# Top-k attention and a gated feed-forward in one kernel: the reciprocal sums are turned by a DMA transpose instead of TensorE

## The chip, the cores and the metric

The kernel runs on one core of one Trainium2 chip. A core has a matrix engine (TensorE, PE in the profile; its weight loads are PEld), a vector engine (VectorE, DVE), an activation engine (ScalarE, ACT), a general engine (GpSimd, POOL) and a queue processor that here issues nearly all DMAs (SyncE, SP). Each runs its own instruction list in order[...]. The metric is the device time of one execution in microseconds (us). Before the change it is 1482.66 us, the median of 3 runs (1482.02 to 1483.18).

## The reference

Two blocks in a row. The attention block has 8 batches of 8 heads, 576 positions and head size 64:

```python
scores = scale * np.matmul(q, k.transpose(0, 1, 3, 2))
kth = np.partition(scores, -top_k, axis=-1)[..., -top_k:-top_k + 1]   # top_k = 32
scores = np.where(scores >= kth, scores, -1000000000.0)
attn = np.exp(scores - np.max(scores, axis=-1, keepdims=True))
attn = attn / (np.sum(attn, axis=-1, keepdims=True) + 1e-09)
attn_out = np.matmul(attn, v)
```

Its output, laid out as 4608 tokens of 512 features, goes through a feed-forward block: `h = x @ w_in` (512 to 2048), `g = h / (1 + exp(-1.702 h))`, `out = g @ w_out` (2048 to 512). All is float32.

## The kernel before, in words

**Slots.** The attention work is cut into 144 slots of 128 query rows by two heads: per batch 16 full slots (four row blocks by four head pairs) and two slots of tails, each of 64 rows of two head pairs. A slot goes through these steps, each on another engine: scores on TensorE (L283), copied to SBUF by ScalarE (L295); the 32 largest of each row by VectorE, with eight-at-a-time maxima and replacements (L345, L348), after the two halves of a row are paired into a larger and a smaller one (L324 on VectorE, L327 and L328 on GpSimd); the bounds of the row by GpSimd (L378); masking and exponentials on ScalarE (L398, L401), which also leave the sum of each row; a copy that parts the float32 probabilities into 16-bit halves (L471); a DMA to DRAM (L473) and a transposing DMA back (L479), which gives `pt`, the probabilities with keys on the partitions; the product with v on TensorE (L539, `values_at`).

**The sums.** The product is made with unnormalised probabilities, so it has to be multiplied by the reciprocal of the row sums, which by then lie along the columns. `sums_of` keeps the sums of a pair of slots in one small tile, 128 x 4. `invert` adds 1e-9 (L430), takes the reciprocal (L432), and lets GpSimd repeat each of the four numbers 64 times into `wide` (L434); `sum_rows` turns `wide` on TensorE, one 128x128 transpose for each slot (L528), into the same PSUM tile `o` that the products go to. ScalarE copies `o`, sums and products together, to SBUF as `x` (L924), and GpSimd multiplies the two parts into the feed-forward's input `xT` (L553, `x_of`).

**The feed-forward.** Four head pairs of one row block make a tile of 128 tokens, which `finish_x` appends to the list `ready`. `hidden` takes the first of that list and makes 512 of its 2048 hidden features (L587, 32 matrix instructions); ScalarE applies tanh (L604) and copies h (L607), GpSimd gates (L616, L617), and `project` multiplies by `w_out` (L635, 8 matrix instructions), four of which add up to one output tile (L641 to SBUF, L643 to DRAM).

**The order.** It is written out by hand (a manual schedule): an engine runs its instructions in the order in which the functions below are called. Slots 0 to 12 go one at a time (`slot`, with another way of turning the probabilities). From slot 13 on `two_slots(n)`, n odd, is called once for every two slots, called a round here. 66 of the rounds finish a pair of slots. In a round, in program order: loads that are due (`begin`); bounds, exponentials and split of slot n-1; the top-k of slot n (`find(n)`, with `invert` of the pair before inside it, after the ninth operation); one `hidden`, one `project`; in 24 of the rounds `prepare_by_dma`, which splits a pair of q and k (L241) and sends it out by four DMAs (L245, L249, L250); the two transposes of `sum_rows`; the scores of slot n+2; the products of slots n-3 and n-2 (`values_at`); the transposing DMA of slot n-1 and, after `prepare_by_dma`, that of q and k (L254); scores of n+3; then more due loads, the bounds and exponentials of slot n, with the copy of `o` and the multiplications `x_of` between them; the split and the transposing DMA of slot n; a second `hidden` and `project`; and the top-k of slot n+1. The SP queue takes its DMAs in just this order, and one that waits holds back all behind it.

**Buffers.** The pool `raws` has 8 buffers that rotate among `lesser`, `wide`, `h`, `x` and others; `ptp` has two (`pt`); `ps_t`, in PSUM, has two (`o` and one `ph`).

Of the kernel before, what the change touches and what calls it, by code (L numbers as in the profile page):

```python
# [11 lines left out]
F32 = mybir.dt.float32  # L12
U32 = mybir.dt.uint32
I32 = mybir.dt.int32
U16 = mybir.dt.uint16
PSUM = bass.MemoryType.PSUM
DRAM = bass.MemoryType.DRAM

P = 128
# [11 lines left out]
def kernel(  # L31
# [27 lines left out]
    nc = tc.nc  # L59

    B, H, S, D = q.shape
# [29 lines left out]
    pool = lambda name, bufs, **kw: ctx.enter_context(tc.tile_pool(name=name, bufs=bufs, **kw))  # L91
# [11 lines left out]
    thp = pool("thp", 5)  # L103
    apart = pool("apart", 4, space=DRAM)
    apart_qk = pool("apart_qk", 2, space=DRAM)
    ps_s = pool("ps_s", 2, space=PSUM)
    ps_t = pool("ps_t", 2, space=PSUM)
    ps_h = pool("ps_h", 1, space=PSUM)
# [309 lines left out]
    def sums_of(n):  # L418
# [3 lines left out]
            sums[k] = small.tile([P, 2, 2], F32, name="sums")  # L422
        return sums[k][:, n % 2, :]

    def invert(n):

        k = n // 2
        if k in sums:
            total = sums[k][:]
            nc.vector.tensor_scalar_add(total, total, 1e-9)  # L430
            inverse = small.tile([P, 4], F32, name="inverse")
            nc.vector.reciprocal(inverse[:], total.rearrange("p s j -> p (s j)"))  # L432
            wide = sums[k] = raws.tile([P, 2, 2, D], F32, name="wide", tag="raw")
            nc.gpsimd.tensor_copy(  # L434
                out=wide[:].rearrange("p s j d -> p (s j) d"),
                in_=inverse[:].unsqueeze(2).to_broadcast([P, 4, D]),
            )

    def turn(n, first, blocks):
        pr = st[n]["pr"]  # L440
# [82 lines left out]
            put_off.append(bring)  # L523


    def sum_rows(m, to):

        nc.tensor.transpose(to, sums[m // 2][:, m % 2, :, :], ident[:])  # L528

    def values_at(m, o):  # L530

        b, t, hps = slots[m]
# [12 lines left out]
                    )  # L545
        st[m].clear()

    def x_of(m, o, by):

        b, t, hps = slots[m]  # L550
        for p in range(2 if t == NF else 1):
            cols = slice(p * TAIL, (p + 1) * TAIL) if t == NF else slice(0, P)
            nc.gpsimd.tensor_tensor(out=x_at(b, t, hps[p]), in0=o[:, cols], in1=by[:, cols], op=ALU.mult)  # L553
        finish_x(m)
# [297 lines left out]
    def two_slots(n):  # L852

        first, second = [later.pop(m, []) for m in (n, n + 1)]
        live = lambda m: 0 <= m < N
        aside = n < N

        def begin(todo):
            for fn, args in todo:
                if fn is not prepare and fn is not prepare_by_dma:  # L860
                    fn(*args)

        def prepare_some(todo):
            for fn, args in todo:
                if fn is prepare or fn is prepare_by_dma:
                    fn(*args)

        def find(m):
            for i, op in enumerate(topk_of_pairs(m) if live(m) else [lambda: None] * 23):
                op()  # L870
                if i == 8 and m % 2:
                    invert(m - 2)
                if i > 1 and unfinished:
                    finish_one()

        def project_one():
            if may_project(0):
                project(True)

        def measure(m):  # L880
            if live(m):
                bounds(m)
            gate(aside)

        opens = n == SETTLED + 1
        begin(first)
        measure(n - 1)
        if opens:
            scores(n + 2)
            bring_all()  # L890
        if live(n - 1):
            exponentials(n - 1)
            split(n - 1)
        if opens:
            copy_scores(n + 2)
            tanh(aside)
        find(n)
        hidden(ps_t if opens else None)
        project_one()
        tanh(aside)  # L900
        prepare_some(first)
        held = [m for m in (n - 3, n - 2) if live(m) and "rows" in st[m]]
        o = ps_t.tile([P, 2, 2, P], F32, name="o", tag="tp") if held else None
        for i, m in enumerate(held):
            sum_rows(m, o[:, i, 0, :])
        if live(n + 2) and not opens:
            scores(n + 2)
            copy_scores(n + 2)
        leave_all()
        for i, m in enumerate(held):  # L910
            values_at(m, o[:, i, 1, :])
        if live(n - 1):
            turn_by_dma(n - 1)
        while turns:
            turns.pop(0)()
        if live(n + 3):
            scores(n + 3)
        begin(second)
        measure(n)
        def bring():  # L920
            if not held:
                return
            x = raws.tile([P, 2, 2, P], F32, name="x", tag="raw")
            nc.scalar.copy(out=x[:], in_=o[:])  # L924
            for i, m in enumerate(held):
                x_of(m, x[:, i, 1, :], x[:, i, 0, :])

        if live(n):
            exponentials(n, bring)
        else:  # L930
            bring()
        if live(n):
            split(n)
            turn_by_dma(n)
        hidden(ps_t)
        if live(n + 3):
            copy_scores(n + 3)
        tanh(aside)
        prepare_some(second)
        project_one()  # L940
        leave_all()
        find(n + 1)
# [41 lines left out]
```

## Time and profile before

| | |
|---|---|
| median of 3 runs | 1482.66 us |
| the profiled execution: its time, its span | 1482.51 us, 1480.7 us |
| PE busy | 1442.7 us (97%) |
| DVE busy | 1382.9 us (93%) |
| ACT busy | 1177.6 us (80%) |
| POOL busy | 859.2 us (58%) |
| L528, transposes of the sums: matrix instructions, mean | 132, 273 ns |
| L434, GpSimd's repeat: instructions, mean | 66, 396 ns |
| L924, copy of `o`: instructions, mean | 66, 585 ns |
| packets of the DMA queue, share of 16 engines | 61.6% |

The span runs from the first to the last instruction of the profiled execution; its time has 1.8 us more around it. A mean is the time of one instruction from its start to its end: matrix instructions overlap, so that a row of them takes less than their number times the mean, and the chain of work that ended last shows what each adds. "Busy" of an engine counts an instruction that is blocked inside as well. The releaser that stands beside an idle time is the instruction whose end let the engine go on.

### The profile page before, as it was taken

To read this page: it belongs to the slowest core of one execution; us is meant where nothing else is said; L and a number is where in the kernel's file an instruction comes from. 1 tells how busy PE (TensorE), PEld (TensorE's weight loads), DVE (VectorE), ACT (ScalarE), POOL (GpSimd) and SP (SyncE) were. 2 spreads that over 40 slices of the span, in tenths; PEclk is the share of its full clock that TensorE was granted. 3 is DMA by queue.
4 is the path that set the end of the run, shared out by engine and by line. 5 is a ranking of instruction groups with operands and counts; after the bars stand their busy time and mean duration, and the time that the engine had idled before them with its cause. 6 is when DMAs were issued, how large, how long until landed. Compare 5 with 4: busy or idle time off the path is not lost.

```text
span 1480.7 us, 31436 instructions
## 1 busy us (share of the span) xinstructions
PE 1442.7 (97%) x10784; PEld 1056.0 (71%) x10784; DVE 1382.9 (93%) x4541; ACT 1177.6 (80%) x1865; POOL 859.2 (58%) x1119
## 2 busy tenths in 40 slices
PE   7789899999999999999999999999999999999998
PEld 5667656777777777777777777777777777777776
DVE  7999989999999999999999999999999999999920
ACT  7998688878788887888878797888878798777730
POOL 3777545566655665666656556665565566665610
PEclk8899999999999999999999999999999999999999
DMA  8451256767667676776678686675767766545430
GB/s 245 135 156 51 72 159 180 202 172 179 173 181 201 159 196 179 178 189 178 170 180 200 168 193 171 183 195 163 179 175 203 174 187 184 140 131 132 127 87 15
DMA packets 516321, 242.20 MB, mean 164 GB/s; under 512 B 452672, under 2 KB 490560, under 8 KB 516160
## 3 DMA queue, kind: packets, MB, share of 16 engines
q1 hardware_dynamic: 515728, 239.89, 61.6%
q8 instruction: 85, 1.39, 0.4%
q14 instruction: 76, 0.62, 0.1%
q10 hardware_dynamic: 432, 0.30, 0.1%
HBM read 45.09 MB, written 102.24 MB: 99 GB/s over the span
## 4 chain that ended last, share of the span: by engine, by line
PE 88%; DVE 10%; ACT 2%; issue 0%; POOL 0%; POOLq 0%; ACTq 0%; DVEq 0%
PE ph L587 34%; PE po L635 32%; PE o L539 10%; PE s_ps L283 10%; DVE top L305 4%; DVE left L308 3%; PE o L528 1%; DVE top L345 1%; PE tp L449 1%; DVE wout L153 0%; DVE left L348 0%; PE none L170 0%; DVE greater L324 0%; ACT pr L401 0%; DVE win L153 0%
## 5 line engine op out<-in xcount | busy, mean ns | idle before, releaser
L635 PE MATMUL po<-wout,th 128*128 128x512 f32 x1152 | 518.6, 593 | 1.1 <-ACT ob L641 1.1
L587 PEld LDWEIGHTS ph<-xT,win 128*128 128x128 f32 x4096 | 472.1, 192 | 53.8 <-issue 52.2
L587 PE MATMUL ph<-xT,win 128*128 128x128 f32 x4096 | 484.4, 277 | 0.0
L635 PEld LDWEIGHTS po<-wout,th 128*128 128x128 f32 x1152 | 208.0, 190 | 211.0 <-issue 208.5
L345 DVE MAX8 top<-left 128x8 f32<-128x288 f32 x792 | 325.2, 445 | 0.0
L471 ACT COPY sc<-pr 128x2304 uint16<-128x2304 uint16 x132 | 278.8, 2112 | 4.2
L295 ACT ACTIVATE sc<-s_ps 128x576 f32<-128x576 f32 x288 | 170.9, 646 | 130.2 <-PE s_ps L283 130.2
L328 POOL TENSOR_TENSOR lesser<-lesser,greater 128x576 int32<-128x576 int32 x132 | 186.2, 1411 | 126.5 <-DVE greater L324 126.3
L348 DVE MATCH_REPLACE8 left<-top,left 128x288 f32<-128x288 f32 x528 | 229.6, 442 | 0.0
L401 ACT ACTIVATE pr<-sc,low 128x576 f32<-128x576 f32 x288 | 220.7, 772 | 0.0
L398 ACT ACTIVATE sc<-sc,cut 128x576 f32<-128x576 f32 x288 | 207.2, 772 | 12.4 <-DVE cut L357 5.8
L345 DVE MAX8 top<-lesser 128x8 f32<-128x288 f32 x528 | 213.5, 444 | 0.0
L327 POOL TENSOR_TENSOR lesser<-sc 128x576 int32<-128x576 int32 x132 | 187.0, 1417 | 2.4 <-ACT sc L295 2.4
L283 PE MATMUL s_ps<-qk_t 64*128 64x288 f32 (+1 forms) x1280 | 183.2, 433 | 0.3 <-ACT qk_t L219 0.3
L617 POOL TENSOR_TENSOR th<-th,h 128x512 f32<-128x512 f32 x128 | 163.7, 1279 | 10.7
L378 POOL TENSOR_SCALAR low<-cut,top 128x1 f32<-128x1 f32 x264 | 65.7, 265 | 175.6 <-DVE cut L357 174.1
L324 DVE TENSOR_TENSOR greater<-sc 128x576 f32<-128x576 f32 x132 | 153.8, 1165 | 11.7 <-ACT sc L295 5.5
L539 PE MATMUL o<-pt,v_l 128*64 128x128 f32 (+1 forms) x2368 | 144.4, 265 | 0.0
L539 PEld LDWEIGHTS o<-pt,v_l 128*64 128x64 f32 x2368 | 120.6, 138 | 25.7 <-issue 22.9
L604 ACT ACTIVATE th<-ph 128x512 f32<-128x512 f32 x144 | 85.9, 596 | 54.9 <-PE ph L587 48.3
L283 PEld LDWEIGHTS s_ps<-qk_t 64*128 64x128 f32 (+1 forms) x1280 | 99.4, 178 | 41.0 <-issue 23.1
L348 DVE MATCH_REPLACE8 left<-top,greater 128x288 f32<-128x288 f32 x264 | 114.7, 442 | 0.0
(86 smaller groups left out, 1535.7 us busy)
## 6 DMA issues: line engine op xcount, KB each, us to landing
rows<-sc SPq DMA_DIRECT2D x132, 576.0 KB, 3.2
qk_rows<-halves SPq DMA_DIRECT2D x48, 256.0 KB, 2.8
qk_l<-in_q_dram SPq DMA_DIRECT2D x64, 128.0 KB, 2.9
raw<-in_moe_w_in_dram SPq DMA_DIRECT2D x16, 512.0 KB, 4.9
v_l<-in_v_dram SPq DMA_DIRECT2D x32, 256.0 KB, 3.1
raw<-in_moe_w_out_dram SPq DMA_DIRECT2D x16, 512.0 KB, 3.5
out_dram<-ob SPq DMA_DIRECT2D x32, 256.0 KB, 2.9
qk_l<-in_k_dram SPq DMA_DIRECT2D x62, 128.0 KB, 2.9
```

The source lines that it names most:

```text
L283: nc.tensor.matmul(ps[i][rows, c, 0:HALF], lhsT=qT[b, hps[p]][on, cols], rhs=kT[b, hps[p]][on, FIRST[i] + c * HALF : FIRST[i] + (c + 1) * ...
L295: nc.scalar.mul(out=to, in_=ps[i][:, :, 0:HALF], mul=SCALE)
L327: nc.gpsimd.tensor_tensor(out=whole, in0=a.bitcast(I32), in1=b.bitcast(I32), op=ALU.add)
L328: nc.gpsimd.tensor_tensor(out=whole, in0=whole, in1=greater[n][:].bitcast(I32), op=ALU.subtract)
L345: nc.vector.max(found(r, i, True), src[:, i, :])
L348: nc.vector.match_replace(to[:, i, :], found(r, i), src[:, i, :], LOWEST)
L398: nc.scalar.activation(sc[:, i, :], sc[:, i, :], AF.Prelu, bias=cut[:, i : i + 1], alpha=HUGE)
L401: nc.scalar.activation(pr[:, i * S : (i + 1) * S], sc[:, i, :], AF.Exp, bias=low[:, i : i + 1], accum_out=den[:, i : i + 1],)
L471: nc.scalar.copy(out=halves, in_=pr[:].bitcast(U16).rearrange("p (k h) -> p h k", h=2))
L539: nc.tensor.matmul(o[j * D : (j + 1) * D, cols], lhsT=main[:, j, c, :] if c < NF else tail[:, j, :], rhs=pt[:, MAIN[j] + c if c < NF else ...
L587: nc.tensor.matmul(ph[:, i * tiles * P : (i + 1) * tiles * P], lhsT=win[:, c, f * P : (f + 1) * P], rhs=xT[c], start=(c == 0), stop=(c == ...
L635: nc.tensor.matmul(po[:], lhsT=gT[:, i * P : (i + 1) * P], rhs=wout[:, f, :], start=(f == 0), stop=(f == FC - 1))
```

## The change

The reciprocal of the pair's four sums is still taken by VectorE and repeated by GpSimd, but as 16-bit halves: `wide` is now 128 x 512 of 16 bits instead of 128 x 256 of 32. A DMA writes it to a new DRAM tile (`by_rows`, pool `apart_by`, two buffers), and a transposing DMA (`turn_inverses`) brings it back as `by_t`, with the numbers of both slots along the columns, interleaved. `x_of` multiplies by `by_t` from there. `sum_rows` and its two transposes are gone, and the PSUM tile `o`, the copy of it and `x` are half as wide. `invert` moves too: it was called in `find` of the odd slot n, after the ninth operation, for the pair finished one round earlier; it is now called in `find` of the even slot n+1, after the seventeenth operation (the two first maxima of the smaller halves, behind `pair_up`), for the pair of the same round. The write to DRAM is the last DMA of a round; the transposing one stands behind `values_at`, before that of slot n-1, in the next round.

```diff
+    inverses = {}
+
     def invert(n):
         k = n // 2
-        if k in sums:
-            total = sums[k][:]
-            nc.vector.tensor_scalar_add(total, total, 1e-9)
-            inverse = small.tile([P, 4], F32, name="inverse")
-            nc.vector.reciprocal(inverse[:], total.rearrange("p s j -> p (s j)"))
-            wide = sums[k] = raws.tile([P, 2, 2, D], F32, name="wide", tag="raw")
-            nc.gpsimd.tensor_copy(
-                out=wide[:].rearrange("p s j d -> p (s j) d"),
-                in_=inverse[:].unsqueeze(2).to_broadcast([P, 4, D]),
-            )
+        if k not in sums:
+            return
+        total = sums.pop(k)[:]
+        nc.vector.tensor_scalar_add(total, total, 1e-9)
+        inverse = small.tile([P, 4], F32, name="inverse")
+        nc.vector.reciprocal(inverse[:], total.rearrange("p s j -> p (s j)"))
+        wide = raws.tile([P, 2, 2, 2, D], U16, name="wide", tag="raw")
+        nc.gpsimd.tensor_copy(
+            out=wide[:],
+            in_=inverse[:].bitcast(U16).rearrange("p (s j h) -> p s h j", s=2, h=2).unsqueeze(4).to_broadcast([P, 2, 2, 2, D]),
+        )
+        rows = inverses[k] = apart_by.tile([P, 2, 2, P], U16, name="by_rows")
+        nc.sync.dma_start(rows[:], wide[:].rearrange("p s h j d -> p s h (j d)"))
+
+    def turn_inverses(n):
+        rows = inverses[n // 2]
+        by = inverses[n // 2] = raws.tile([P, P, 2], F32, name="by_t", tag="raw")
+        nc.sync.dma_start_transpose(
+            out=by[:].rearrange("p q s -> p (q s)").bitcast(U16), in_=rows[:].rearrange("q s h c -> (q s h) c")
+        )
...
-    def sum_rows(m, to):
-        nc.tensor.transpose(to, sums[m // 2][:, m % 2, :, :], ident[:])
...
-    def x_of(m, o, by):
+    def x_of(m, o):
         b, t, hps = slots[m]
+        by = inverses[m // 2][:, :, m % 2]
...
         def find(m):
...
-                if i == 8 and m % 2:
-                    invert(m - 2)
+                if i == 16 and m % 2 == 0:
+                    invert(m - 1)
...
-        o = ps_t.tile([P, 2, 2, P], F32, name="o", tag="tp") if held else None
-        for i, m in enumerate(held):
-            sum_rows(m, o[:, i, 0, :])
+        o = ps_t.tile([P, 2, P], F32, name="o", tag="tp") if held else None
...
         for i, m in enumerate(held):
-            values_at(m, o[:, i, 1, :])
+            values_at(m, o[:, i, :])
+        if held:
+            turn_inverses(n - 2)
         if live(n - 1):
             turn_by_dma(n - 1)
...
-            x = raws.tile([P, 2, 2, P], F32, name="x", tag="raw")
+            x = raws.tile([P, 2, P], F32, name="x", tag="raw")
             nc.scalar.copy(out=x[:], in_=o[:])
             for i, m in enumerate(held):
-                x_of(m, x[:, i, 1, :], x[:, i, 0, :])
+                x_of(m, x[:, i, :])
```

More of the change, by code (lines that the diff above doesn't have):

```diff
@@ L105 @@
     apart_qk = pool("apart_qk", 2, space=DRAM)
+    apart_by = pool("apart_by", 2, space=DRAM)
     ps_s = pool("ps_s", 2, space=PSUM)
```

## The prediction, made before the changed kernel was run

> **What bounds the kernel now.** I read the busy times by stretch first, then the chain of work that ended last, then the timeline of one round (one call of `two_slots`) engine by engine. Between 240 and 1400 us TensorE is busy in all of every 40 us and VectorE in 39.3 to 39.6, so either could be the limit. The chain decides: 88% of it is PE. Of its order in time, one whole round:
>
> ```profile
> 610.42 0.22 PE o L528 x2
> 610.64 1.17 PE s_ps L283 x8
> 611.81 2.33 PE o L539 x40
> 614.14 1.17 PE s_ps L283 x8
> 615.31 3.77 PE ph L587 x32
> 619.08 3.44 PE po L635 x8
> 622.52 3.57 PE ph L587 x32
> 626.09 3.44 PE po L635 x8
> 629.52 0.22 PE o L528 x2
> ```
>
> The columns are start, length, engine, tile, line and count. A round lasts 19.10 us (610.42 to 629.52), all of it TensorE with no hole, and L528, which the change removes, is 0.22 us of it: not two means of 273 ns, since matrix instructions overlap.
>
> Why does VectorE, nearly full, not appear? From the timeline, around the multiplication that makes `xT`:
>
> ```profile
> 652.46 0.58 ACT L924 COPY x<-o 128x512 f32<-128x512 f32 x1
> 653.12 0.88 POOL L553 TENSOR_TENSOR xT<-x 128x128 f32<-128x128 f32 x2 [1.48 <-ACT x L924]
> 653.41 2.83 PE L587 MATMUL ph<-xT,win 128*128 128x128 f32 x23
> 653.95 1.41 POOL L327 TENSOR_TENSOR lesser<-sc 128x576 int32<-128x576 int32 x1
> 654.46 1.51 DVE L324 TENSOR_TENSOR greater<-sc 128x576 f32<-128x576 f32 x1
> ```
>
> L324 takes 0.76 us in the first half of nearly every round, but 1.4 to 2.0 in the second, where it starts while GpSimd's L327 runs and ends some 0.6 us after it. L327 follows `x_of`, `x_of` the copy L924, and that TensorE's products. So VectorE is held to TensorE's pace by this stretch of about 0.85 us; alone it would need 19.10 - 0.85 = 18.25 us a round.
>
> The same lines show the tight place. The second `hidden` (653.41) starts 0.29 us after `x_of` does. Each block of `xT` it takes costs two L587, 3.57/32 x 2 = 0.22 us; the two blocks from this round are the third and fourth, needed at about 653.9 and 654.1; they are ready at 653.56 and 654.0. Matching `ready` by its order with the starts of L587, nine tiles are used like this, in the round that makes them (starts 233, 271, 309, 348, 577, 615, 653, 692 and 921 us). All others wait 15 us or more, a round of TensorE's work.
>
> The DMAs by line, kilobytes and median us from issue to landing, and what SP waits for:
>
> ```profile
> rows<-sc SPq DMA_DIRECT2D x132, 576.0 KB, 3.2
> pt<-rows SPq DMA_TRANSPOSE x132, 4.6
> qk_rows<-halves SPq DMA_DIRECT2D x24, 64.0 KB, 2.5
> SPq L479 <- DMA rows<-sc: 307.4, 109, 4.3
> ```
>
> **What the Trainium skill says.** "SBUF — State Buffer", section "SBUF: two separate sides": VectorE and GpSimd share a port pair under an exclusive lock, held for a whole instruction, which also covers a VectorE operation with two SBUF inputs against a GpSimd one that reads SBUF. L324 against L327 agrees (0.76 against 1.51 us). "DMA: Bandwidth & Descriptors", section "Rules for kernel authors": a DMA that reads what another wrote must wait for its completion. The trace agrees: that wait alone is 307.4 us of SP in 109 times, and the change adds one more per round. "Advanced Engine Details and Errata", section "X-Bar Transpose (TRN2)": transposing DMAs are as fast as plain ones. Only partly here: 4.6 us against 3.2 for the same bytes, and the difference lies near the 2.05 to 3.5 us (median 2.49) that SP spends issuing it, against 0.39.
>
> **The change part by part.**
>
> *TensorE.* Two transposes go: -0.22 us a round. In the first three of the 66 rounds other engines lead (below); 63 x 0.22 = -13.9 us. Removing them hides nothing and frees nothing else on TensorE; the weight loads lie under the matrix instructions.
>
> *ScalarE.* L924 is half as wide: about -0.24 us (0.585 to some 0.35, as the 128x384 and 128x128 copies take 0.478 and 0.256 us). ScalarE is 80% busy, so this is worth nothing by itself, but `x` is ready 0.24 us earlier.
>
> *VectorE.* L430 and L432, 0.35 us, move from the first half to the second, one pair earlier. In the steady rounds the sums wait for nothing: the exponentials of slot n end about 2.2 us after the products, the new place comes 4.4 us after. Behind it stand 20 operations of the next cut, and 0.85 us of slack cover 0.35.
>
> *GpSimd.* The repeat is 512 elements, not 256: 0.62 us by L616's 128x512 (617 ns), between 0.40 (L434, if 16-bit elements go twice as fast) and 1.2. It leaves the first half and comes after L328 in the second, where GpSimd now idles 1.3 us waiting for the cut, so I take nothing.
>
> *SP.* Two DMAs more a round. The write is 128 KB: 0.45 us of issue (L473 and L245: 0.33 to 0.6), 2.5 to 2.8 to landing by the rows above. The transpose has 128x512 elements where `pt` has 128x2304: 2.49 x 512/2304 = 0.55 us of issue, floor 0.35, ceiling 2.5 if the count matters little; landing 2.2 us after the issue ends (`pt`: 4.6 - 2.49), so about 2.8 in all, 2.5 to 5. SP's other transposes are at the earliest 1 us from being late: `pt` of slot n lands some 3 us or more before its product.
>
> *The new wait.* `x_of` now also waits for `by_t`. The write leaves after SP's last transpose, about 10.3 us after the products (12.5 beside a transpose of q and k), lands 2.7 later, and in ordinary rounds the transpose lands 1 to 2 us before `x_of` wants it: nothing. In two kinds of round SP is late. With q and k loads due, six loads and often three of v hold SP until the split's DMA is out (e.g. 649.32 + 0.59, products done at 652.28). With 0.5 us for the new write, `by_t` is issued at 650.4 and lands at 653.2 to 653.7. With `prepare_by_dma`, four DMAs go first (to 612.35, products at 614.07), and it lands at 615.2 to 616. Both are 1 to 2 us after the products, where `x_of` used to start 0.84 after. Behind `x_of` on GpSimd stand L327, L328, the repeat, the bounds, and the gate (1.41 + 1.41 + 0.62 + 0.50 + 1.90 = 5.84 us); TensorE wants the gated tile only 11.95 us after the products, so `x_of` may end 6.1 after and costs nothing, except for the nine tiles used at once. All nine are in rounds of these two kinds. There `x_of` must start by 0.95 us after the products; `by_t` comes at 0.9 to 2.3. I take 0.6 us each, 9 x 0.6 = +5.4, from 0 to 1.5 each (+13.5).
>
> *The start.* In the round that begins near 176 us the new place of `invert` meets unfinished exponentials:
>
> ```profile
> 198.91 0.81 DVE L345 MAX8 top<-lesser 128x8 f32<-128x288 f32 x2
> 199.11 0.76 ACT L401 ACTIVATE pr<-sc,low 128x576 f32<-128x576 f32 x1
> 199.78 0.19 ACT L401 ACTIVATION_READ_ACCUMULATOR pr<-sc,low 128x1 f32 x1
> ```
>
> VectorE could start L430 at 198.07 and would wait until 199.97, here on the chain (196.66 to 219). With 0.34 us from L528 and 0.24 from the copy that is 1.67 us, minus 0.68 for two rounds' L528 on the same chain (0.34 each, where they don't overlap): +1.0. One round earlier the wait is 5.4 us (174.4 to 179.8), but 0.85 and 4.62 us of waits for scores swallow it.
>
> Sum: -13.9 + 5.4 + 1.0 = -7.5, from 1482.51 (span 1480.7 and 1.8 around it): 1475.0. The median, 1482.66, stands 0.15 higher; I keep 1475.
>
> *Buffers.* `raws` hands out seven a round instead of six, from eight. Each is then taken when its holder one round and one place earlier is done; the tightest is `h`, after the last read of `lesser`, some 6 us before. No wait.
>
> **The rivals.** (1) *Hidden entirely.* `by_t` lands within 0.95 us of the products in the nine rounds too, or VectorE runs ahead: where `x_of` is late, L324 comes before L327 and loses its stretch, later cuts and DMAs come earlier. For it: 0.63 us of slack remains per round. Time 1482.5 - 13.9 + 1.0 = 1469.6. (2) *Eaten.* 1.3 to 1.5 us at each of nine tiles, or a slower start by some us: 1480 to 1485, no measurable change.[...] (3) *Slower: the transpose lands over 5.2 us after the products.* Then `x_of` ends past 6.1, the gate is late, and TensorE waits in every round before L635. It takes an issue of 2.5 us plus a landing of 5, in a round with `prepare_by_dma`, or a queue pushed back by 3 us. From there each us costs 24 us over such rounds, 63 over all: 1 us too much in all gives 1482.5 - 12.9 + 63 = 1533, in those 24 alone 1494. Against it: 3 us of margin. (4) *The change doesn't do what it says*: excluded for TensorE, as L528 is gone from its list.
>
> **How the numbers follow.** 0.50 for the forecast (1471 to 1479), 0.22 for hidden, 0.14 for eaten, 0.14 for slower. About 0.2% (3 us) is what a measurement of this kernel can tell from no change, so faster means under 1479.7: nearly all of the first and all of the second, 0.70; same 0.16; slower 0.14. The range runs from 1468.5, just under hidden, to 1485, the end of eaten, leaving out the slow rival and a little on either side.
>
> **What would show it.** Steady rounds of 18.88 us away from the nine tiles; L528 absent and L283 straight after L635; the add of the sums waiting near 198 us, for ScalarE; `x_of` waiting for the transpose in the rounds with loads or `prepare_by_dma`; holes of 0 to 1.5 us before or within nine L587 groups; the second L324 stretched by some 0.6 instead of 0.85 us. I am wrong if TensorE waits before L635 or L539, if a round stays at 19.1, if the small transpose takes SP over 1 us or over 4 to land, or if VectorE waits for the sums beyond the start.

## The result, and the profile after

The changed kernel takes 1498.43 us, the median of 4 runs (1497.07 to 1500.81), against 1482.34 us (1481.94 to 1483.18) for the kernel before, measured beside it: a ratio of 1.011, 95% interval 1.0092 to 1.0127. It is slower by 16 us where 7.5 us less were forecast, and it lies beyond the range. Every median here is of fast executions: one of a later variant, 2346 us at a mean clock of 0.575, is left out.

I compare the profiled spans, 1495.2 and 1480.7 us. Rounds go by the n of `two_slots(n)`, so their numbers are odd. A round is measured from the end of its products (the last L549, called V below) to that of the next round's. Between round 19 and round 139, 60 rounds, this takes 1157.8 us where it took 1146.6 before: +11.2. Up to V of round 19 it is 235.2 against 231.9: +3.3. The tail is the same to 0.01 us. The +11.2 has two parts. A round without a stall is 18.88 us long, as forecast, which is 0.22 less in each: 60 x 0.22 = -13.2. The other rounds are longer by 25.0 us in all, where before it was 0.6: +24.4.

The start of the page, the rows of parts 5 and 6 that answer to those of before, and the share of the DMA queue:

```profile
span 1495.2 us, 31457 instructions
...
PE 1442.0 (96%) x10652; PEld 1046.7 (70%) x10652; DVE 1359.5 (91%) x4541; ACT 1163.3 (78%) x1865; POOL 885.8 (59%) x1119
...
q1 hardware_dynamic: 561136, 257.20, 66.1%
...
L564 POOL TENSOR_TENSOR xT<-x,by_t 128x128 f32<-128x128 f32 x116 | 56.2, 505 | 268.5 <-DMA by_t<-by_rows 193.3
...
L325 DVE TENSOR_TENSOR greater<-sc 128x576 f32<-128x576 f32 x132 | 115.5, 875 | 9.3 <-ACT sc L296 9.3
...
rows<-sc SPq DMA_DIRECT2D x132, 576.0 KB, 3.3
...
by_rows<-wide SPq DMA_DIRECT2D x66, 128.0 KB, 2.4
```

PE is as busy as before (1442.7) although 132 of its instructions are gone. That is a warning: busy time that stays while work leaves is work that ran slower. The row to look at is L564, the multiplication `x_of` (L553 before): GpSimd stood 193.3 us before it for the new transpose. By itself that proves no loss, since GpSimd is not the bound. The view of waits says whether it reaches TensorE:

```profile
POOL xT L564 <- DMA by_t<-by_rows: 193.3, 38, 7.8
...
DVE sums L434 <- ACT pr L402: 42.5, 34, 5.8
...
PEld ph L598 <- POOL xT L564: 13.6, 13, 3.1
...
PE ph L598 <- POOL xT L564: 10.9, 7, 2.9
```

After the line come the us in total, the times, and the longest. `by_t` is late 38 times for full tiles (5 more for those of tails), but TensorE's `hidden` (L598) waits for `xT` only 7 times, 10.9 us in all. The rest of the 24.4 must lie elsewhere. Round 27, the costliest, shows where, in the timeline:

```profile
312.99 0.37 ACT L935 COPY x<-o 128x256 f32<-128x256 f32 x1
...
313.39 1.63 SPq L449 DMA_TRANSPOSE by_t<-by_rows  x1
...
313.95 0.71 PE L598 MATMUL ph<-xT,win 128*128 128x128 f32 x4
...
317.05 0.87 POOL L564 TENSOR_TENSOR xT<-x,by_t 128x128 f32<-128x128 f32 x2 [5.73 <-ACT sc L485]
...
317.56 6.31 PE L598 MATMUL ph<-xT,win 128*128 128x128 f32 x28 [2.90 <-POOL xT L564]
```

The products end at 312.89. `by_t` is issued only at 313.39; `x_of` starts at 317.05, which is V + 4.16 us. (The releaser named there, L485, happens to end in the same tenth of a us; `x_of` needs nothing of it. The transpose took 3.5 us from issue to landing, to 316.9.) TensorE takes four L598 for the blocks that it has, stands 2.90 us, and then needs 6.1 us (317.56 to the next L646 at 323.70) for 28 matrix instructions, which at the pace of a quiet round take 28 x 0.115 = 3.2. The busy times by stretch say why. The first two numbers are the length of the stretch and TensorE's busy time in it; the last three are TensorE's granted clock, the DMA share and GB/s:

```profile
313.47:316.88 3.41, 1.19 (x16) 0.56 (x8) 3.38 (x13) 3.38 (x5) 0.00 (x0) 1.00 0.76 227
316.88:323.71 6.83, 6.15 (x29) 6.15 (x30) 6.76 (x25) 1.23 (x3) 4.67 (x7) 0.50 0.62 175
```

From 316.88 to 323.71 the clock is 0.50. A stall of 2.9 us has cost 6.0. Round 55 is the same: TensorE stood 1.80 us and lost 3.9. Round 99 stood 2.65 us, kept a clock of 1.00 and lost 3.0.

The excess of all rounds over 18.88 us, from the timelines, sorted by what is in the round:

| kind of round | rounds | excess, us |
|---|---|---|
| loads of q and k; the tile is used at once | 19, 27, 55, 63, 91, 99 | 0.85, 6.01, 3.90, 2.00, 1.22, 3.03 = 17.0 |
| `prepare_by_dma`; the tile is used at once | 23, 31, 59, 67, 95, 103 | 1.27, 0.54, 0.30, 0.73, 0.45, 0.59 = 3.9 |
| the last tiles, used at once | 127, 131, 135 | 0.28, 0.31, 0.28 = 0.9 |
| gate late behind a late `x_of` | 33, 39, 75, 111, 121 | 1.38, 0.21, 0.33, 0.47, 0.52 = 2.9 |
| the other 40 | | 0.3 |

Round 139, the last that uses a tile at once, loses 0.47 and lies behind the window, in the tail. Of rounds 31, 67, 103 and 121, 0.15 us each is no loss of the change: they are as much longer in the kernel before and in the first experiment.

### The profile page after: what moved, and what is told of

The parts are those of the page before. It is cut to its first block, busy times and chain, and to the rows that moved or that the text cites. A ratio compares the mean times of both kernels' runs of the same rounds, so it can differ in the third digit from the quotient of the medians.

```text
span 1495.2 us, 31457 instructions
## 1 busy us (share of the span) xinstructions
PE 1442.0 (96%) x10652; PEld 1046.7 (70%) x10652; DVE 1359.5 (91%) x4541; ACT 1163.3 (78%) x1865; POOL 885.8 (59%) x1119
## 5 line engine op out<-in xcount | busy, mean ns | idle before, releaser
L598 PEld LDWEIGHTS ph<-xT,win 128*128 128x128 f32 x4096 | 478.7, 193 | 69.1 <-issue 51.8
L646 PE MATMUL po<-wout,th 128*128 128x512 f32 x1152 | 519.1, 593 | 2.5 <-POOL th L628 1.3
L598 PE MATMUL ph<-xT,win 128*128 128x128 f32 x4096 | 495.0, 279 | 11.2 <-POOL xT L564 10.9
L646 PEld LDWEIGHTS po<-wout,th 128*128 128x128 f32 x1152 | 208.1, 190 | 213.2 <-issue 208.8
L346 DVE MAX8 top<-left 128x8 f32<-128x288 f32 x792 | 320.9, 446 | 0.0
L485 ACT COPY sc<-pr 128x2304 uint16<-128x2304 uint16 x132 | 278.8, 2112 | 4.2
L564 POOL TENSOR_TENSOR xT<-x,by_t 128x128 f32<-128x128 f32 x116 | 56.2, 505 | 268.5 <-DMA by_t<-by_rows 193.3
L328 POOL TENSOR_TENSOR lesser<-sc 128x576 int32<-128x576 int32 x132 | 194.2, 1471 | 0.0
L628 POOL TENSOR_TENSOR th<-th,h 128x512 f32<-128x512 f32 x128 | 165.3, 1292 | 10.7
L549 PE MATMUL o<-pt,v_l 128*64 128x128 f32 (+1 forms) x2368 | 145.3, 266 | 0.1
L549 PEld LDWEIGHTS o<-pt,v_l 128*64 128x64 f32 x2368 | 121.3, 138 | 27.2 <-issue 24.6
L325 DVE TENSOR_TENSOR greater<-sc 128x576 f32<-128x576 f32 x132 | 115.5, 875 | 9.3 <-ACT sc L296 9.3
```

The source lines that it names most:

```text
L328: nc.gpsimd.tensor_tensor(out=whole, in0=a.bitcast(I32), in1=b.bitcast(I32), op=ALU.add)
L346: nc.vector.max(found(r, i, True), src[:, i, :])
L485: nc.scalar.copy(out=halves, in_=pr[:].bitcast(U16).rearrange("p (k h) -> p h k", h=2))
L549: nc.tensor.matmul(o[j * D : (j + 1) * D, cols], lhsT=main[:, j, c, :] if c < NF else tail[:, j, :], rhs=pt[:, MAIN[j] + c if c < NF else ...
L598: nc.tensor.matmul(ph[:, i * tiles * P : (i + 1) * tiles * P], lhsT=win[:, c, f * P : (f + 1) * P], rhs=xT[c], start=(c == 0), stop=(c == ...
L646: nc.tensor.matmul(po[:], lhsT=gT[:, i * P : (i + 1) * P], rhs=wout[:, f, :], start=(f == 0), stop=(f == FC - 1))
```

## The experiments

The theory: **lateness**. `by_t` comes late because its issue stands behind other DMAs on SP; TensorE stops in the rounds that use the tile at once, and its clock makes that dearer. The rivals: **traffic** (two more DMAs a round slow the other DMAs, or SP, whoever waits for them); **lost cover** (with L325 moved out of GpSimd's way VectorE runs ahead and now waits for the sums, 42.5 us in 34 places); and the **start** alone.

**No transpose, no write.** The repeat stays where the change put it and in GpSimd's hands, but `x_of` multiplies by it unturned. The expectation says what is left out.

```diff
-        rows = inverses[k] = apart_by.tile([P, 2, 2, P], U16, name="by_rows")
-        nc.sync.dma_start(rows[:], wide[:].rearrange("p s h j d -> p s h (j d)"))
...
-        by = inverses[m // 2][:, :, m % 2]
+        by = wides[m // 2][:, m % 2, :, :, :].rearrange("p j d h -> p (j d h)").bitcast(F32)
...
-        if held:
-            turn_inverses(n - 2)
```

> The changed kernel without its two new DMAs: the repeated reciprocals stay where GpSimd wrote them and x_of multiplies by them as they lie, so the turn of the sums is left out and the output is not the reference's. It shows what the loss of the two TensorE transposes and the move of invert are worth alone. Theory A (by_t is late for tiles that TensorE uses at once, and TensorE's clock halves after the stall): 22 us of stalls go, the start still costs 3: 1473 to 1477 us. Rival B (the new DMAs crowd SP and the DMA engines, so that other transfers are late): 1470 to 1477 too. Rival C (VectorE's wait for the sums, 42.5 us in 34 rounds, sets the loss): no gain, 1494 to 1499.

Measured: 1471.65 us (1470.29 to 1474.39), ratio 0.993 (0.9914 to 0.9945). A little below the 1473 to 1477 expected: the start costs 1.5 us here, not 3 (V of round 19 at 233.4). The 60 rounds are 18.88 us each, with 0.7 us of excess in all. What the change removes is worth what the prediction said, and the whole loss in the rounds comes with the two DMAs.

**Both DMAs, but no wait for them.** The write and the transpose are issued as in the changed kernel; nobody reads `by_t`.

```diff
-        nc.sync.dma_start(rows[:], wide[:].rearrange("p s h j d -> p s h (j d)"))
+        nc.sync.dma_start(rows[:].rearrange("p s h c -> p (s h c)"), wide[:].rearrange("p s j d h -> p (s j d h)"))
...
-        by = inverses[m // 2][:, :, m % 2]
+        by = wides[m // 2][:, m % 2, :, :, :].rearrange("p j d h -> p (j d h)").bitcast(F32)
```

> The changed kernel with both new DMAs in their places, but x_of multiplies by the repeated reciprocals as GpSimd wrote them and never reads by_t, so the turn is left out of the result (the repeat is written with a stride of two). It has the load on SP and the DMA engines without the wait. Theory A: 1473 to 1478 us, within 2 us of the kernel without the DMAs. Rival B: most of the loss stays, 1490 or more. Rival C: 1494 to 1499.

Measured: 1474.25 us (1468.56 to 1474.56), ratio 0.9933 (0.9909 to 0.9958), excess of the rounds 3.6 us. So the DMAs themselves cost at most some 3 us (the executions of the two kernels overlap), and the wait for `by_t` 24 us (1498.43 - 1474.25). Traffic falls as the main cause. Lost cover falls too, as the main cause: L325 is free of GpSimd here as well (772 ns in the mean, 875 in the changed kernel, 1165 before), so VectorE is ahead, and the rounds still take 18.88 us. Its wait for the sums has shrunk to 6 places in the view of waits:

```profile
DVE sums L434 <- ACT pr L402: 13.7, 6, 5.8
```

Most of VectorE's 34 waits in the changed kernel come with the lateness of `by_t` and go with it; they are no cause of their own. But the lost cover has a small price. The 2.9 us by which the rounds are longer here than without the DMAs lie nearly all in nine of the rounds that use a tile at once, about 0.3 us in each, though `x_of` starts at V + 0.55 there. Its second multiplication ends late, as in the changed kernel's round 131 (products end at 1316.90):

```profile
1317.45 1.47 POOL L564 TENSOR_TENSOR xT<-x,by_t 128x128 f32<-128x128 f32 x2 [2.42 <-ACT x L935]
1317.86 0.74 DVE L325 TENSOR_TENSOR greater<-sc 128x576 f32<-128x576 f32 x1
...
1318.97 2.64 PEld L598 LDWEIGHTS ph<-xT,win 128*128 128x128 f32 x23 [0.23 <-POOL xT L564]
```

The two multiplications take 1.47 us instead of 0.88: the second one is due at V + 0.97, just behind the start of L325, and ends 0.32 us after L325 does. Wherever such a pair takes over 1.0 us in this trace and the changed kernel's, L325 was running when one of its multiplications was due. It is the stretch of L324 and L327 in the prediction, with the roles exchanged: the earlier VectorE is, the more it is GpSimd that is held. What places L325 just there in these rounds was not tested.

**`invert` at its old place.** The write then leaves in the first half, close ahead of the transpose, instead of at the end of the round before.

```diff
-                if i == 16 and m % 2 == 0:
-                    invert(m - 1)
+                if i == 8 and m % 2:
+                    invert(m - 2)
```

> One part of the change undone: invert is called again in find of the odd slot, after the ninth operation, for the pair of the round before; the two DMAs stay. Theory A: the start gets its 3 us back, but the write to DRAM now leaves in the same round as the transpose that reads it, so SP waits for it and by_t comes no earlier: 1493 to 1502 us. Rival C: VectorE waits for no sums any more, so most of the loss goes: 1470 to 1480 us.

Measured: 1514.08 us (1511.46 to 1518.17), ratio 1.0216 (1.0194 to 1.0238); excess of the rounds 44.4 us. That is above the 1493 to 1502 expected, and far from the 1470 to 1480 of lost cover. Where nothing stands between the two DMAs on SP, the transpose now waits for the write to land (issued at 669.78 and 672.67 us in one round). Later still is worse still, and moving `invert` was on the whole a gain of the change, not its loss. In its view of waits GpSimd waits longer for the transpose, and TensorE for GpSimd:

```profile
POOL xT L564 <- DMA by_t<-by_rows: 240.2, 44, 9.4
...
PEld ph L598 <- POOL xT L564: 23.3, 9, 4.8
...
PE ph L598 <- POOL xT L564: 21.7, 7, 4.6
```

**The transpose earlier.** `turn_inverses` is issued right behind the split of slot n-1, ahead of `prepare_by_dma`'s four DMAs, and the round's first loads are moved behind it.

```diff
-        begin(first)
         measure(n - 1)
...
             split(n - 1)
+        held = [m for m in (n - 3, n - 2) if live(m) and "rows" in st[m]]
+        if held:
+            turn_inverses(n - 2)
+        begin(first)
...
-        if held:
-            turn_inverses(n - 2)
```

> The changed kernel with the transposing DMA of by_t issued right behind the split of slot n-1, before the four DMAs of prepare_by_dma, and with the loads of a round moved behind it. Nothing else is changed. Theory A: by_t lands 1 us or more before x_of wants it, the stalls at the tiles used at once go, the start's 3 us stay: 1474 to 1478 us. Rival B: the load is the same, 1490 or more. Rival C: 1494 to 1499.

Measured: 1474.04 us (1473.79 to 1476.79), ratio 0.9948 (0.9933 to 0.9962): faster than both kernels. Excess of the rounds 6.0 us, at most 0.73 in any of the twelve with loads or `prepare_by_dma`. Round 27 here, in the timeline:

```profile
305.23 1.15 SPq L449 DMA_TRANSPOSE by_t<-by_rows  x1
...
307.46 0.37 ACT L935 COPY x<-o 128x256 f32<-128x256 f32 x1
...
308.15 0.88 POOL L564 TENSOR_TENSOR xT<-x,by_t 128x128 f32<-128x128 f32 x2
...
308.42 3.84 PE L598 MATMUL ph<-xT,win 128*128 128x128 f32 x32
```

The transpose leaves 2.1 us before the products end (307.36), `x_of` starts at V + 0.79, and the 32 L598 run through. Both DMAs, their issue and their traffic are still there; only their place has changed. This is the main proof of lateness.

**Only the loads behind it.** The transpose stays behind `values_at`; the loads move behind the transpose.

```diff
-        begin(first)
         measure(n - 1)
...
         if held:
             turn_inverses(n - 2)
+        begin(first)
```

> The changed kernel with the loads of a round's first half moved behind the transposing DMA of by_t, which stays where the change put it, behind the four DMAs of prepare_by_dma. Theory A, as the rounds of the changed kernel are counted: the six rounds with loads that use a tile at once lose 17 us, the six with prepare_by_dma 3.4: 1479 to 1484 us. If SP's order before by_t were not the cause, 1494 or more.

Measured: 1483.8 us (1480.6 to 1486.53), ratio 1.0008 (1.0 to 1.0017). The six load rounds lose nothing worth the name (0.1 us at most, against 17.0 in all); the six with `prepare_by_dma`, where SP's order is unchanged, lose 8.6 (1.87, 1.48, 2.31, 1.03, 0.91, 1.03). So loads ahead of the transpose are what made the large stalls, and `prepare_by_dma` ahead of it makes the small ones. These grew from 3.9 to 8.6, with `x_of` at V + 1.2 to 3.1 instead of V + 1.1 to 2.1. In rounds 23, 31, 59 and 95 SP comes to the round late, behind the loads that the round before now issues later: the split's DMA, first in the round, leaves at V - 4.7 to V - 3.5 instead of V - 7.7 to V - 7.1. In rounds 67 and 103 the transpose is issued as before (V - 1.53), and what they lose more goes with a second multiplication of `x_of` that stands beside L325 (it ends at V + 2.60, in the changed kernel at 2.29 and 2.15).

**The tile handed on later.** The tiles of a round join the list `ready` only behind the round's second `hidden`, so that none is used at once.

```diff
-    def x_of(m, o):
+    def x_of(m, o, late):
...
-        finish_x(m)
+        late.append(m)
...
         hidden(ps_t)
+        for m in late:
+            finish_x(m)
```

> The changed kernel, its DMAs where the change put them, but a finished tile enters the list ready only behind the round's second hidden, so that no tile is used in the round that makes it. by_t is as late as before. Where the list is empty the second hidden has nothing to do, and about one hidden and one project (7 us) go to the end. Theory A: by_t's lateness no longer stops TensorE: 1479 to 1487 us. If by_t's lateness costs through GpSimd's queue (the gate) rather than through the tiles used at once, it stays at 1495 or more.

Measured: 1490.72 us (1486.02 to 1491.43, three executions), ratio 1.0048 (1.003 to 1.0066). This is above the 1479 to 1487 expected. The excess of the rounds falls from 25.0 to 8.6 us, but 7.0 of the fall is work put off: in round 19 the list is empty, and one `hidden` and one `project` go to the tail, which grows by 7.0. So 15.6 us of waits are left in the rounds: taking the tiles out of reach saves 9.4 us, and not the 22 that they cost, as TensorE then stands at the gate instead. With no tile used at once, nearly all of the 15.6 lies in rounds where `x_of` is very late, and there TensorE stops before L646. Round 93, GpSimd's timeline first (products end at 935.32):

```profile
942.21 0.88 POOL L564 TENSOR_TENSOR xT<-x,by_t 128x128 f32<-128x128 f32 x2 [8.89 <-DMA by_t<-by_rows]
943.05 1.41 POOL L328 TENSOR_TENSOR lesser<-sc 128x576 int32<-128x576 int32 x1
944.54 1.40 POOL L329 TENSOR_TENSOR lesser<-lesser,greater 128x576 int32<-128x576 int32 x1
945.89 0.60 POOL L438 COPY wide<-inverse 128x512 uint16<-128x512 uint16 x1
946.48 0.99 POOL L379 TENSOR_SCALAR low<-cut,top 128x1 f32<-128x1 f32 x2
947.44 0.61 POOL L627 TENSOR_SCALAR th<-th 128x512 f32<-128x512 f32 x1
948.14 1.26 POOL L628 TENSOR_TENSOR th<-th,h 128x512 f32<-128x512 f32 x1
```

and TensorE's:

```profile
943.54 3.73 PE L598 MATMUL ph<-xT,win 128*128 128x128 f32 x32
949.46 5.40 PE L646 MATMUL po<-wout,th 128*128 128x512 f32 x8 [2.19 <-POOL th L628]
```

Behind `x_of` stands the whole list that the prediction counted (L328 to the gate, L628); the gate ends at 949.40, and L646 waits 2.19 us for it, then runs slowly (5.40 us instead of 3.60). Set side by side over the changed kernel and the experiments, the start of `x_of` after V and the excess of rounds in which no tile was used at once are: 4.77 us and 0.33; 4.99, 0.47; 5.40, 1.38; 5.48, 1.14 (this kernel); 6.18, 1.79 (next one); 6.88, 4.15 (this round). Up to some 4.7 us lateness is free, then it costs roughly one for one (0.51 at 5.46 and 2.23 at 6.66 in this kernel show the scatter), and more where the clock falls, as it does behind this stall (0.50 from 949.97 to 953.38).

**The second `project` ahead of the second `hidden`.** That gives `xT` 3.4 us more, and takes them from the gate.

```diff
+        project_one()
         hidden(ps_t)
...
         tanh(aside)
         prepare_some(second)
-        project_one()
```

> The changed kernel with the second project of each round ahead of the second hidden on TensorE, instead of behind it: by_t gets 3.4 us more until its tile is used, and the gate of that hidden 3.4 us less. Theory A: the stalls at the tiles used at once shrink from 22 us to under 5; a new wait for the gate before the first project of the next round may cost up to 0.3 us a round: 1474 to 1492 us.

Measured: 1483.12 us (1479.75 to 1486.34), ratio 1.0007 (0.9999 to 1.0016). The excess falls to 13.0 us; none of the twelve rounds loses more than 0.52, although `x_of` starts at V + 2.4 to 4.7 in eleven of them, and the largest losses are now at gates (1.79 with `x_of` at V + 6.18 and V + 6.21, 1.50 at V + 5.87). The `by_t` of this kernel is no earlier than that of the changed one; more cover alone brings 15.3 us back.

**The start alone.** `invert` at its old place for the first two pairs only.

```diff
+    FIRST_PAIRS = 15
...
-                if i == 16 and m % 2 == 0:
+                if i == 8 and m % 2 and m - 2 <= FIRST_PAIRS:
+                    invert(m - 2)
+                if i == 16 and m % 2 == 0 and m - 1 > FIRST_PAIRS:
                     invert(m - 1)
```

> The changed kernel, with invert at its old place for the first two pairs only (slots 12 to 15), and at the new one for all others. Theory A: of the loss only the start's 3 us come back: 1493 to 1497 us. If the start's stall also sets the phase in which later rounds run, more comes back: under 1490.

Measured: 1496.21 us (1493.35 to 1496.47), ratio 1.0088 (1.0072 to 1.0103). The way from V of round 15 to V of round 19, 34.1 us before and 37.5 in the changed kernel, is 34.6 here, 2.9 less; 2.2 of it show in the time. So the start is worth 2 to 3 us of the 16, and is no rival to lateness. Part of it is the clock: it is 0.50 for 6.83 us in that stretch here, for 10.24 in the changed kernel.

**Both repairs.** The earlier transpose, and `invert` as in the last kernel for the first two pairs (there the transpose stays behind `values_at`).

```diff
-        begin(first)
...
+        early = bool(held) and (n - 2) // 2 in inverses
+        if early:
+            turn_inverses(n - 2)
+        begin(first)
...
-        if held:
+        if held and not early:
             turn_inverses(n - 2)
```

> The early transposing DMA (behind the split, ahead of prepare_by_dma and of the loads) together with invert at its old place for the first two pairs. Theory A: both losses go, 1482.5 - 0.22 x 63 = 1468.6, some us more for what is left of late DMAs: 1468 to 1473 us, faster than the kernel before and than the early transpose alone.

Measured: 1475.65 us (1473.16 to 1476.94), ratio 0.9954 (0.9942 to 0.9967). Above the 1468 to 1473 expected, and not better than the earlier transpose alone. The start gains (34.3 us from round 15 to 19, 35.8 without the second repair), but round 23 loses 2.42 with `x_of` at V + 2.90. V of round 15 lies anywhere between 195.5 and 198.4 us in the profiled executions, in no order that the edits give, so a gain of 1.5 us at the start can't be told by spans.

**The stall filled.** To see what the clock costs, TensorE is given useless products of the identity with itself just ahead of the stalls of rounds 27 (12 of them) and 55 (8).

```diff
-    def hidden(into=None):
+    def hidden(into=None, fill=0):
...
+        for _ in range(fill):
+            nc.tensor.matmul(ph[:, 0:P], lhsT=ident[:], rhs=ident[:], start=True, stop=True)
...
-        hidden(ps_t)
+        hidden(ps_t, {27: 12, 55: 8}.get(n, 0))
```

> The changed kernel, with useless 128x128 products on TensorE in front of the second hidden of two rounds: 12 (2.7 us) in round 27, where TensorE stood 2.9 us, and 8 (1.8 us) in round 55, where it stood 1.8. They write into the hidden's own PSUM tile, which is overwritten after, and wait for nothing. If the halved clock behind those two stalls (6.0 and 3.9 us lost for 2.9 and 1.8 us of standing) comes from the standing, these two rounds lose 3 and 2 us instead, and the kernel 5 us less: 1493 us. If it has another cause, the useless products change nothing or add their own time: 1498 to 1503.

Measured: 1503.92 us (1502.3 to 1507.91), ratio 1.0157 (1.014 to 1.0173). In the two rounds it did what it should. Round 27, TensorE's timeline, with `x_of` as late as in the changed kernel (V + 4.23 against V + 4.16):

```profile
313.69 2.94 PE L597 MATMUL ph<-ident 128*128 128x128 f32 x24
316.47 0.61 PE L600 MATMUL ph<-xT,win 128*128 128x128 f32 x4
317.37 3.59 PE L600 MATMUL ph<-xT,win 128*128 128x128 f32 x28 [0.29 <-POOL xT L564]
320.80 3.60 PE L648 MATMUL po<-wout,th 128*128 128x512 f32 x8
```

(L600 and L648 are L598 and L646.) The 28 take 3.4 us up to L648, not 6.1, and the clock of this stretch is 1.00:

```profile
317.40:320.90 3.50, 3.50 (x29) 3.38 (x30) 3.46 (x15) 0.45 (x1) 3.42 (x4) 1.00 1.06 291
```

The round loses 3.36 us instead of 6.01, with the same lateness: 2.65 us of round 27 were the clock's. Round 55 loses 2.02 instead of 3.90, of which 0.25 is an earlier `x_of` (V + 2.85 against 3.10). But the kernel as a whole is slower, because other rounds came out worse: 63 lost 4.26, 67 2.03, and 99 6.68 us with `x_of` at V + 4.81, against 2.00, 0.73 and 3.03. In 63 and 99 the clock fell this time, to 0.50 for 3.41 and 6.83 us. How late `by_t` is in a round depends on where SP's queue stands, and this shifts when an earlier stall changes its length; the forecast of the total assumed that it stays.

## Why the prediction was wrong, point by point

**Right.** L528's worth: 0.22 us a round, to the hundredth, and without the DMAs the kernel takes 1471.65, close to the 1469.6 of the rival *hidden entirely*. The repeat takes 610 ns on GpSimd (0.62 forecast), the narrower copy L935 371 ns (0.35). VectorE's wait near 198 us and the one a round earlier, 5.4 us, came as forecast, in its timeline:

```profile
180.38 0.17 DVE L434 TENSOR_SCALAR sums<-sums 128x4 f32<-128x4 f32 x1 [5.35 <-ACT pr L402]
...
199.70 1.08 DVE L434 TENSOR_SCALAR sums<-sums 128x4 f32<-128x4 f32 x1 [1.16 <-ACT pr L402]
```

Four of its signs of being wrong appeared too: the small transpose takes SP over 1 us (1.35) and up to 5.5 us to land, TensorE's weight loads wait for the gate before L646 (2.2 us in all), and VectorE waits for the sums beyond the start (34 places).

The mechanism of the main cost was right: `x_of` waits in rounds with loads or `prepare_by_dma`, and TensorE stops in the tiles used at once. Its sum was not: 5.4 us were forecast, and the sixteen rounds that use a tile at once cost 22.2 (17.0 + 3.9 + 0.9 + 0.47).

**Wrong: "nine tiles are used like this".** They are sixteen. The matching of `ready` with the starts of L587 missed the rounds 95, 99, 103 and the last four. Those seven cost 0.45 + 3.03 + 0.59 + 0.87 + 0.47 = 5.4 us.

**Wrong: "I take 0.6 us each".** That is what the rounds with `prepare_by_dma` lose (3.9/6 = 0.65). Those with loads lose 17.0/6 = 2.8, beyond the ceiling of 1.5. Two terms made it so. The small transpose was to be issued in 2.49 x 512/2304 = 0.55 us; it took 1.35 in the median, and the shortest 1.14, in the view of its tile:

```profile
L449 SPq DMA_TRANSPOSE by_t<-by_rows x66: 1142/1353/2545, 191.6 to 1441.7; - x66
...
DMA to landing us min/median/max: 2.4/3.3/5.5
```

An issue of 2.49 us for 2304 elements and 1.35 for 512 isn't proportional: a straight line through the two medians has a fixed part of 1.0 us (an estimate from these two sizes). The prediction had the other end ("ceiling 2.5 if the count matters little") but took its value from the lower one. And "lands at 653.2 to 653.7", 0.9 to 1.4 us after the products, supposed that it is issued 1.9 us before they end. In round 27 it was issued 0.5 us after their end, since SP's queue had fallen behind TensorE: the write before it started at 307.12, and six loads behind it held SP until 312.70:

```profile
307.12 1.57 SPq L443 DMA_DIRECT2D by_rows<-wide  x1
308.73 1.30 SPq L186 DMA_DIRECT2D qk_l<-in_q_dram  x2
310.08 0.63 SPq L189 DMA_DIRECT2D qk_l<-in_q_dram  x1
310.75 1.28 SPq L186 DMA_DIRECT2D qk_l<-in_k_dram  x2
312.07 0.63 SPq L189 DMA_DIRECT2D qk_l<-in_k_dram  x1
312.80 0.54 SPq L487 DMA_DIRECT2D rows<-sc  x1
313.39 1.63 SPq L449 DMA_TRANSPOSE by_t<-by_rows  x1
```

The write itself took 1.57 us to issue there (0.53 in the median), and `by_t` took 3.5 us from issue to landing, with the 576 KB of the split just ahead of it (5.5 in round 55). So the term "`by_t` comes at 0.9 to 2.3" after the products was too small: it lands as late as V + 5.3 (round 33). It is late in four of the six ordinary rounds of the stretch too (35, 53, 71, 89, 107, 125; `x_of` starts at up to V + 2.51), where no wait was forecast; there it costs nothing. Moving the loads behind the transpose is worth 14.6 us (1498.4 - 1483.8), moving the transpose ahead of `prepare_by_dma` as well 24.4.

**Missing: the clock.** The prediction took a stall at its length. The halved clock doubled it in rounds 27 and 55 (2.9 to 6.0, 1.8 to 3.9), about 5 us in the two. It did not in round 99, although TensorE stood 2.65 us there. The traces show what parts the two cases. The clock changes only at times that are whole multiples of 3.413 us apart in a trace, so the stretches at 0.50 behind the opening are 3.41, 6.83 or 10.24 us long. Cut at these times, round 55 and then round 99 look like this:

```profile
586.54:589.95 3.41, 1.61 (x11) 1.25 (x10) 2.82 (x13) 3.38 (x6) 1.36 (x3) 1.00 0.16 33
589.95:593.36 3.41, 3.41 (x18) 3.41 (x17) 3.41 (x14) 0.77 (x2) 3.32 (x5) 0.50 0.98 240
...
1009.79:1013.20 3.41, 1.93 (x24) 1.03 (x20) 3.38 (x13) 3.38 (x7) 0.00 (x0) 1.00 0.74 222
1013.20:1016.61 3.41, 2.25 (x18) 2.13 (x19) 3.34 (x14) 1.97 (x3) 2.68 (x4) 1.00 0.93 231
```

In round 55 all 1.80 us of standing lie in one window of 3.41 us, and the clock is 0.50 in the next; in round 99 a window's end parts the 2.65 us into 1.48 and 1.17, and the clock stays. Over the twelve traces (this kernel, the one before and the ten experiments), from 190 to 1440 us, the clock fell at the end of 25 windows, with 1.80 us or more of standing in each; in the 4318 others at full clock TensorE stood 1.78 us at most. In the opening, before 190 us, the two groups overlap. This is a count over traces; the one experiment on it is the filled stall.

So whether a stall of 2 to 3 us is doubled is luck of its place among these windows, and a window at half clock costs up to 1.7 us. Over the whole span the clock shows as 0.983 after and 0.989 before: 0.017 x 1495.2 - 0.011 x 1480.7 = 9 us of TensorE's time, the opening's part in it.

**Too small: the start, +1.0.** It is +3.3. The two waits were right, but L434, a 128x4 addition that took 0.15 us before, stood 1.08 us in the second of these rounds and 0.92 in the next, while GpSimd was running; and TensorE, which then stands 5.60 us instead of 2.97, goes on with half its clock:

```profile
228.00:235.00 7.00, 6.99 (x49) 5.84 (x48) 6.93 (x27) 3.13 (x8) 1.90 (x3) 0.50 0.73 191
```

Before, it was 0.76 in the stretch from 226 to 233. The moved `invert` brings the longer stall: TensorE stands 5.6 to 5.7 us in seven of the eight kernels that have it in all rounds, 3.0 to 3.3 in the four that have the old place there; L434's share of that was not tested. The rest is again the place among the windows: with a stall of 5.7 us, the way from V of round 15 to V of round 19 is 35.7 to 35.8 us in three experiments where the clock is 0.50 for 6.83 us (one of them the kernel without the DMAs), and 37.1 to 37.5 in the changed kernel and three experiments where it is 0.50 for 10.24 us. So about 1.5 us of the start is luck.

**The slower rival, and what it missed.** Its mechanism (a late gate) is real, and its point of decision, a start of `x_of` at V + 5.2, was nearly right (the cost begins near V + 4.7). It came into play in five rounds and cost 2.9 us. Its price, "each us costs 24 us over such rounds", was meant for all rounds with `prepare_by_dma` at once; lateness is not that even. The 14% for slower stood on this mechanism; what decided was the forecast's own mechanism with the cost of its tiles used at once four times too small, which no rival had. *Eaten* came nearest, 1.3 to 1.5 us at each tile, and stopped where the trace of before gave no reason to stop: at the ceiling of an issue estimated too low.

The 0.3 us that the last four tiles lose is L325 beside `x_of`, as above (round 131), and no lateness of `by_t`. Still open: how far SP's queue falls behind from one round to the next, which sets each round's lateness and which no run took apart; and what lengthens the stall at the start.

## What to carry to other kernels

When work moves from an engine to a DMA, its place in the issuing queue decides more than its length: write down for each kind of round what is issued ahead of it and when its consumer wants it, and put a short transfer whose consumer is close ahead of loads whose consumer is far (24 us here, by moving two calls). Count the uses that have no slack from the kernel's own order, not from a few samples, and don't scale a cost with size from one measured size: take it between the scaled value and the whole. Price a stall of TensorE as a range, from its length to twice that, since the clock may fall behind it (here with 1.8 us of standing in one of its windows).

## What the runs showed of the hardware

TensorE's clock fell to 0.50 with stalls of 2.90 and 1.80 us, for 6.83 and 3.41 us. The Trainium skill, "TensorE: Matmul & The Clock Gate", section "Part 1: The HAM clock gate", tells of such halving after an idle window of about 3.4 us, with a window that runs freely. The runs agree in the size (half) and in windows of 3.41 us that don't follow the kernel, but a window need not be idle throughout: in these twelve traces 1.80 us of standing within one was enough, and 1.78 was not.

SP's time for issuing a transposing DMA grows less than its size: 1.35 us in the median (1.14 at least) for 128x512 elements of 16 bits, 2.49 for 128x2304. A tiny VectorE instruction (128x4) is held by GpSimd's work: L434 took 145 ns at best and 1384 at worst, 388 in the mean, and all 18 of its 66 instructions that took over 250 ns ended within 0.1 us of the end of a GpSimd instruction that was running when they started.
